# Attention: each V product as two products in 64-column halves of the array

## The chip, the cores and the metric

The kernel runs on one core of one Trainium2 chip. The metric is the time of one execution on the device in microseconds (us). Before the change two timed runs took 2069.55 and 2069.77 us (median 2069.66).

## The reference

Three stages follow one another. Attention with a block-causal mask of 64 tokens, over 4 batches, 8 heads, 576 tokens and 64 dimensions per head, feeds a layer with a cosine gate, and that feeds eight experts with a Sinkhorn gate. The change touches only the attention:

```python
def _attn_ref(q, k, v):
    B, H, S, D = q.shape                       # 4, 8, 576, 64
    scores = np.matmul(q, k.transpose(0, 1, 3, 2)) / np.sqrt(D)
    ...                                        # mask: block of the query >= block of the key
    scores = scores - np.max(scores, axis=-1, keepdims=True)
    attn = np.exp(scores)
    attn = attn / (np.sum(attn, axis=-1, keepdims=True) + 1e-09)
    return np.matmul(attn, v)
...
x = _moe_ref(x=attention rows, w_in, w_out)    # g = h * cos(h)
return _moe2_ref(x=x, w_gate, w1, w2)          # 8 experts, all of them for every token
```

## The kernel before

The order of all work is written out by hand; each engine runs its instructions in the order of the program. Attention is a loop over the 32 heads (`for i in range(NH)`, L445) and takes the first 191 us. Keys lie on the partitions, in five chunks of 128, and queries on the free axis, so that a product of scores gives, for one chunk of keys, a tile keys x queries. In head i TensorE does, in this order:

- the first part of the row maxima of head i + 1 (`peak`, L291, tile `px`), from rounded q and k;
- the scores of head i (`scores`, L330 and L331, tiles `sp`, `sq`, `sr`, `sc`), which ScalarE turns into weights with exp (L344, tiles `ep`, `eq`, `er`, `ec`);
- `pv(i, 0)`, the V product of the first chunk: two products, of 320 and 256 queries;
- the second part of the maxima (L291 again, two products);
- `pv(i, 1)` and `pv(i, 2)`: products of 128, 320 and 320 queries;
- the transpose of the maxima of head i + 1 (L318, tile `pt`), which waits for VectorE's reductions (L313);
- `pv(i, 3)` and `pv(i, 4)`: products of 192 and 64 queries.

So the V products of a head come in three groups, and between the groups TensorE does products that use the full width of the array. The moving operand of a V product is a tile of weights after exp (keys x queries), the stationary operand is V of that chunk, and the output is (dimension x queries), in PSUM tile `o`, of which there is one buffer. All of it is float32. The scores and everything after the attention run in a rounded form of float32 (`F32R`), with high and low parts.

The sums of the softmax come out of the same product. For an even head the stationary operand is 65 columns wide: V in columns 0 to 63, ones in column 64. For an odd head it is 128 wide: ones in column 0, zeros in 1 to 63, V in 64 to 127. So the output of an even head lies on partitions 0 to 63 with the sums on 64, and that of an odd head on 64 to 127 with the sums on 0; two heads then fill one tile of 128 partitions. `evac` (L360) copies output and sums to SBUF on ScalarE in the next head, before `pv(i, 0)` writes `o` anew.

After the attention there are narrow operands on TensorE too: the products for the gate (L551 and L552, tile `plt`, stationary operand 16 columns wide on 128 rows, rounded float32), a transpose of one column (L968, tile `pmx`, float32) and transposes on 16 rows (L559, tile `plg`, float32). `ones` (L51) is a tile of 128 x 128 ones that is made at the start.

Of the kernel before, what the change touches and what calls it, by code (L numbers as in the profile page):

```python
# [20 lines left out]
B, H, S, D = 4, 8, 576, 64  # L21
# [22 lines left out]
def attention_moe_kernel(ctx: ExitStack, tc: tile.TileContext, qk, v, w_a, gate, w_b, out):  # L44
    nc = tc.nc
# [5 lines left out]
    ones = top.tile([128, 128], F32, name="ones")  # L51
# [100 lines left out]
    def attention():  # L152
        with tc.tile_pool(name="at1", bufs=1) as p1, tc.tile_pool(name="at2", bufs=2) as p2, \
# [16 lines left out]
            V = [p1.tile([128, 5, D + 1], F32, name="v0"), p1.tile([128, 5, 2 * D], F32, name="v1")]  # L170
            VC = [slice(0, D), slice(D, 2 * D)]
# [9 lines left out]
            st, EP, EQ, ER, EC, SUMS, SR, INV, ps_t, ps_o = ({} for _ in range(10))  # L181
# [162 lines left out]
                nc.scalar.activation(E[i], ps[:, 0:n], AF.Exp, scale=0.125)  # L344

            def pv(i, c):
                m = D + 1 if i % 2 == 0 else 2 * D
                if c == 0:
                    ps_o[i] = pso.tile([128, 1024], F32, tag="o", name="o")
                o = ps_o[i][0:m, 256:832]  # L350
                vt = V[i % 2][:, :, 0:m]
                blocks = ((lambda: ((256, 576, EP[i][:, 0:320]), (0, 256, EQ[i][:, 0:256]))),
                          (lambda: ((128, 256, ER[i][:, 0:128]), (256, 576, ER.pop(i)[:, 128:448]))),
                          (lambda: ((256, 576, EC.pop(i)),)),
                          (lambda: ((384, 576, EP.pop(i)[:, 320:512]),)),
                          (lambda: ((512, 576, EQ.pop(i)[:, 256:320]),)))[c]()
                for q0, q1, e in blocks:
                    nc.tensor.matmul(o[:, q0:q1], vt[:, c], e, start=c == 0, stop=True, skip_group_check=c > 0)  # L358

            def evac(i):  # L360
                o, t = ps_o.pop(i)[:, 256:832], RAW[i // 2 % 3]
# [83 lines left out]
            for i in range(NH):  # L445
# [24 lines left out]
                if i % 4 == 2:  # L470
                    some(1)
                pv(i, 0)
                if nxt:
                    find(*peak(i + 1, 1))
# [17 lines left out]
                if i >= NH - 3:  # L492
                    j = i - (NH - 3)
                    f, o = FIRST[j][0], FIRST[j][1] * DM
                    split(*SPARE[j], raw[f][:, o:o + DM], nc.scalar, nc.gpsimd)
                pv(i, 1)
                pv(i, 2)
                if nxt:
                    turn(i + 1)
# [9 lines left out]
            e = NH - 2  # L509
# [7 lines left out]
    with tc.manual_schedule():  # L517
# [795 lines left out]
        tgen, at = None, ""  # L1313
# [11 lines left out]
        for g in range(NG + 2):  # L1325
            now, w = g < NA, Weights(g + 1) if g + 1 < NA else None
            left = NE * NJ - g % (NE * NJ)
            if left == 14 and g + left < NG:
                tgen = tprep(groups[g + left][0], nc.gpsimd)
                at = "sum"  # L1330
# [32 lines left out]
            if now:  # L1363
                if g:
# [3 lines left out]
                c = [fin.tile([128, TB], F32, tag=f"c{i}", name="c") if g else C01[i] if i < 2 else  # L1368
                     post.tile([128, TB], F32, tag="tt", name="c", bufs=3) for i in range(3)]
# [103 lines left out]
```

## Time and profile before

| | |
|---|---|
| timed runs | 2069.55 and 2069.77 us |
| span of the profiled execution | 2069.4 us |
| TensorE (PE) busy, its weight loads (PEld) | 2057.5 us, 1939.8 us |
| VectorE (DVE), ScalarE (ACT), GpSimd (POOL) busy | 1552.5, 1045.1, 830.2 us |
| attention stage | 0 to 191 us |
| line 358 (the V products) in the chain that ended last | 4% of the span |

The profile is of one execution, and times are counted from its first instruction. PE are products, PEld the weight loads ahead of them, which overlap the products. A product's start is measured and its end is modelled, so how long it holds the array is read from the start of what follows it. A float32 product appears as two records, each with a weight load of its own. In a row, `o<-ep,v` says that tile `o` is written from tiles `ep` and `v`; `128*65` is rows x columns of the stationary operand, and `128x320` partitions x elements of the moving one.

### The profile page before, as it was taken

What the parts mean: (1) busy time and instruction counts of PE and PEld (TensorE: products, weight loads), DVE (VectorE), ACT (ScalarE), POOL (GpSimd) and SP (SyncE); (2) the same over time, 40 slices, a digit from 0 to 9 for tenths busy, and PEclk for the clock granted to TensorE, in tenths of its full rate; (3) what the DMA queues carried; (4) which work ended last, traced back from release to release, by engine and by line L of the source; (5) the groups of instructions that cost most, each with busy time, mean ns of one, the idle gap of its engine ahead of it and who ended that gap; (6) DMA issues with size and microseconds to landing.
All of it is one profiled execution on the core that took longest, in us unless ns stands there. A gap on an engine that the chain in (4) does not pass through costs nothing.

```text
span 2069.4 us, 34729 instructions
## 1 busy us (share of the span) xinstructions
PE 2057.5 (99%) x12687; PEld 1939.8 (94%) x12687; DVE 1552.5 (75%) x2731; ACT 1045.1 (51%) x1852; POOL 830.2 (40%) x633
## 2 busy tenths in 40 slices
PE   9999999999999999999999999999999999999998
PEld 8888999999999898889889999999999999999998
DVE  7887786566668788887776777777777777777777
ACT  7887775434454433334333544454445444444443
POOL 4553332333325444455441333344444333333333
PEclk9999999999999999999999999999999999999999
DMA  6774330001035477766567455545555655455553
GB/s 163 186 187 130 117 98 1 6 1 41 1 106 205 160 256 246 255 237 220 204 221 248 165 200 177 207 165 201 179 203 183 210 177 204 165 204 176 197 173 112
DMA packets 177754, 340.89 MB, mean 165 GB/s; under 512 B 42128, under 2 KB 86672, under 8 KB 177584
## 3 DMA queue, kind: packets, MB, share of 16 engines
q1 hardware_dynamic: 177584, 338.68, 48.9%
q8 instruction: 100, 1.64, 0.3%
q14 instruction: 70, 0.57, 0.1%
HBM read 249.11 MB, written 80.36 MB: 159 GB/s over the span
## 4 chain that ended last, share of the span: by engine, by line
PE 92%; issue 4%; POOL 2%; DVE 1%; ACT 0%; POOLq 0%; DVEq 0%; ACTq 0%
PE p L524 8%; PE p L523 7%; PE p L522 7%; PE acc L805 7%; PE hx L522 6%; PE hx L523 6%; PE hx L524 6%; PE acc L522 4%; PE acc L524 4%; PE acc L523 4%; PE o L358 4%; PE hy L522 3%; PE hy L523 3%; PE hy L524 3%; PE h L522 2%
## 5 line engine op out<-in xcount | busy, mean ns | idle before, releaser
L1096 POOL TENSOR_TENSOR w<-s,w 128x512 fp32r<-128x512 f32 x150 | 236.6, 1578 | 408.2 <-ACT w L1095 394.9
L1192 DVE SCALAR_TENSOR_TENSOR oa<-p,P,oa 128x256 f32<-128x256 f32 x648 | 280.7, 477 | 69.5 <-PE p L524 67.9
L524 PE MATMUL p<-w,xl 128*128 128x256 f32 x906 | 255.9, 282 | 1.0 <-DVE xl L1143 1.0
L522 PE MATMUL p<-w,xh 128*128 128x256 f32 x846 | 238.2, 282 | 2.5 <-DVE oa L1192 1.7
L523 PE MATMUL p<-w,xh 128*128 128x256 f32 x846 | 238.4, 282 | 0.0
L638 POOL TENSOR_TENSOR wv<-stg,wv 128x512 fp32r<-128x512 f32 x62 | 111.0, 1811 | 232.1 <-ACT wv L637 225.1
L1096 POOL TENSOR_TENSOR w<-raw,w 128x512 fp32r<-128x512 f32 x74 | 116.6, 1576 | 188.7 <-ACT w L1095 175.5
L524 PEld LDWEIGHTS p<-w,xl 128*128 128x128 f32 x906 | 171.8, 190 | 1.5 <-DVE xl L1143 1.4
L759 POOL TENSOR_TENSOR jl<-raw,jh 128x512 fp32r<-128x512 f32 x63 | 92.3, 1465 | 189.6 <-ACT jh L754 169.6
L522 PEld LDWEIGHTS p<-w,xh 128*128 128x128 f32 x846 | 159.8, 189 | 2.9 <-issue 1.9
L523 PEld LDWEIGHTS p<-w,xh 128*128 128x128 f32 x846 | 160.3, 189 | 0.0
L522 PE MATMUL acc<-wv,hs 128*128 128x512 f32 x384 | 152.9, 398 | 0.0
L524 PE MATMUL acc<-wv,hs 128*128 128x512 f32 x384 | 152.0, 396 | 0.0
L523 PE MATMUL acc<-wv,hs 128*128 128x512 f32 x384 | 151.6, 395 | 0.0
L522 PE MATMUL p<-w,xl 128*128 128x256 f32 x498 | 140.0, 281 | 0.1
L523 PE MATMUL p<-w,xl 128*128 128x256 f32 x498 | 140.1, 281 | 0.0
L1040 DVE SCALAR_TENSOR_TENSOR oa<-acc,P,oa 128x512 f32<-128x512 f32 x168 | 123.8, 743 | 13.4 <-PE acc L524 13.4
L522 PE MATMUL hx<-th,w 128*128 128x384 f32 x384 | 129.6, 338 | 0.7 <-ACT c L1264 0.7
L523 PE MATMUL hx<-tl,w 128*128 128x384 f32 x384 | 129.0, 336 | 0.0
L524 PE MATMUL hx<-th,w 128*128 128x384 f32 x384 | 128.9, 336 | 0.0
L1139 ACT ACTIVATE xh<-raw 128x768 fp32r<-128x768 f32 x141 | 117.6, 843 | 17.3 <-DVE raw L1155 8.5
L524 PE MATMUL p<-w,xh 128*128 128x256 f32 x438 | 123.7, 282 | 0.6 <-DVE xh L1143 0.6
(309 smaller groups left out, 6367.7 us busy)
## 6 DMA issues: line engine op xcount, KB each, us to landing
w<-w1d SPq DMA_DIRECT2D x128, 512.0 KB
w<-w1d SPq DMA_DIRECT2D x128, 384.0 KB
stg<-in_w_b_dram SPq DMA_DIRECT2D x64, 512.0 KB
s<-td SPq DMA_DIRECT2D x86, 256.0 KB
w1d<-wah SPq DMA_DIRECT2D x32, 512.0 KB
w1d<-wal SPq DMA_DIRECT2D x32, 512.0 KB
s<-in_w_b_dram SPq DMA_DIRECT2D x64, 256.0 KB
td<-stg SPq DMA_DIRECT2D x52, 256.0 KB
```

The source lines that it names most:

```text
L358: nc.tensor.matmul(o[:, q0:q1], vt[:, c], e, start=c == 0, stop=True, skip_group_check=c > 0)
L522: nc.tensor.matmul(ps, lh, rh, start=first, stop=False, skip_group_check=go_on)
L523: nc.tensor.matmul(ps, lh, rl, start=False, stop=False, skip_group_check=go_on)
L524: nc.tensor.matmul(ps, ll, rh, start=False, stop=last, skip_group_check=go_on)
L638: eng.tensor_tensor(out=t[:, DM:2 * DM], in0=src, in1=t[:, 0:DM].bitcast(F32), op=ALU.subtract)
L759: eng.tensor_tensor(out=lo, in0=raw[units[n][1]][:, part * DM:(part + 1) * DM], in1=hi.bitcast(F32), op=ALU.subtract)
L805: nc.tensor.matmul(acc[half, b][:, at:at + w_], w[:, s], h[:, t0:t0 + w_], start=f == 0 and i == 0 and at == 0, stop=f == F1 - 1 and i == ...
L1040: nc.vector.scalar_tensor_tensor(out=o, in0=acc, scalar=p, in1=o, op0=ALU.mult, op1=ALU.add)
L1096: nc.gpsimd.tensor_tensor(out=t[:, DM:2 * DM], in0=raw, in1=t[:, 0:DM].bitcast(F32), op=ALU.subtract)
L1139: nc.scalar.activation(self.h[o], self.get(o), AF.Copy)
L1192: nc.vector.scalar_tensor_tensor(out=o, in0=ps, scalar=p, in1=o, op0=ALU.mult, op1=ALU.add)
```

## The change

A product of V is split in two that stream the same moving weights. One has V as its stationary operand, 64 columns, and writes the half of the partitions where the output of that head belongs (0 to 63 for an even head, 64 to 127 for an odd one). The other has 64 columns of `ones` and writes the other half, so that all 64 partitions of that half hold the sums. `evac` is unchanged and reads one of them. The output tile, the blocks and the groups stay as they are. What fills the columns of ones and zeros beside V is still there but no longer read.

```diff
             def pv(i, c):
-                m = D + 1 if i % 2 == 0 else 2 * D
                 if c == 0:
                     ps_o[i] = pso.tile([128, 1024], F32, tag="o", name="o")
-                o = ps_o[i][0:m, 256:832]
-                vt = V[i % 2][:, :, 0:m]
+                o = ps_o[i][:, 256:832]
+                at, of = ((0, D), (D, 2 * D)) if i % 2 == 0 else ((D, 2 * D), (0, D))
+                vt = V[i % 2][:, :, VC[i % 2]]
...
                 for q0, q1, e in blocks:
-                    nc.tensor.matmul(o[:, q0:q1], vt[:, c], e, start=c == 0, stop=True, skip_group_check=c > 0)
+                    nc.tensor.matmul(o[at[0]:at[1], q0:q1], vt[:, c], e, start=c == 0, stop=True,
+                                     skip_group_check=True)
+                    nc.tensor.matmul(o[of[0]:of[1], q0:q1], ones[:, 0:D], e, start=c == 0, stop=True,
+                                     skip_group_check=True)
```

On TensorE, the second and third group of an even head, with the transpose of the maxima between them; `v_109` is the tile of V of the even heads, and a shape is output partitions x queries:

```order
-L358 MATMUL o<-er,v_109 65x128
-L358 MATMUL o<-er,v_109 65x320
-L358 MATMUL o<-ec,v_109 65x320
+L358 MATMUL o<-er,v_109 64x128
+L360 MATMUL o<-er,ones 64x128
+L358 MATMUL o<-er,v_109 64x320
+L360 MATMUL o<-er,ones 64x320
+L358 MATMUL o<-ec,v_109 64x320
+L360 MATMUL o<-ec,ones 64x320
 L318 MATMUL pt<-ident,nm_107 101x128
```

Behind each product with V there is now one with `ones` on the same moving tile (line 360 of the changed kernel). The transpose comes after six products in place of three.

On TensorE, the first group of an odd head, between the last scores and the second part of the maxima; `v_110` is the tile of V of the odd heads:

```order
 L331 MATMUL sc<-qa_100,ka 128x320
-L358 MATMUL o<-ep,v_110 128x320
-L358 MATMUL o<-eq,v_110 128x256
+L358 MATMUL o<-ep,v_110 64x320
+L360 MATMUL o<-ep,ones 64x320
+L358 MATMUL o<-eq,v_110 64x256
+L360 MATMUL o<-eq,ones 64x256
 L291 MATMUL px<-ka,qa_99 128x448
```

Two products over all 128 partitions became four over 64, and a full-width product stands ahead of the group and behind it. No other engine's order changes.

## Rows read from the trace of the kernel before

**Rows 1.** The page, busy time of each engine: us, share of the span, records.
```profile
PE 2057.5 (99%) x12687; PEld 1939.8 (94%) x12687; DVE 1552.5 (75%) x2731; ACT 1045.1 (51%) x1852; POOL 830.2 (40%) x633
```
**Rows 2.** One stretch of the attention: PE, PEld, DVE, ACT, POOL busy; clock, DMA, GB/s.
```profile
50.00:90.00 40.00, 40.00 (x236) 32.91 (x234) 32.76 (x63) 33.06 (x61) 21.14 (x21) 1.00 0.71 187
```
**Rows 3.** Waits on PE's side, 0 to 192 us: total us, times, longest.
```profile
PEld pt L318 <- DVE nm L313: 11.3, 31, 0.4
...
PEld sp L331 <- DVE qa L322: 1.5, 2, 1.0
```
**Rows 4.** The chain that ended last, one head: start us, us, line, records.
```profile
42.64 0.97 PE o L358 x4
...
43.96 1.30 PE o L358 x6
...
45.43 0.49 PE o L358 x4
...
48.24 0.97 PE o L358 x4
```
**Rows 5.** Line 358 by shape, 0 to 192 us: records, busy us, mean ns, idle before.
```profile
L358 PEld LDWEIGHTS o<-er,v 128*128 128x128 f32 x64 | 9.0, 191 | 0.3
...
L358 PEld LDWEIGHTS o<-er,v 128*65 128x65 f32 x64 | 7.9, 137 | 0.4
...
L358 PE MATMUL o<-ec,v 128*128 128x320 f32 x32 | 11.2, 433 | 0.0
L358 PE MATMUL o<-ec,v 128*65 128x320 f32 x32 | 11.2, 433 | 0.0
```
**Rows 6.** V products in order of time, one even head: start us, us, records.
```profile
59.31 0.70 PE L358 MATMUL o<-ep,v 128*65 128x320 f32 x2
59.85 0.59 PE L358 MATMUL o<-eq,v 128*65 128x256 f32 x2
...
60.63 0.92 PE L358 MATMUL o<-er,v 128*65 128x128 f32 x4
61.38 0.70 PE L358 MATMUL o<-ec,v 128*65 128x320 f32 x2
...
62.09 0.49 PE L358 MATMUL o<-ep,v 128*65 128x192 f32 x2
62.42 0.28 PE L358 MATMUL o<-eq,v 128*65 128x64 f32 x2
```
**Rows 7.** Weight loads in order of time, the same head.
```profile
60.06 0.41 PEld L291 LDWEIGHTS px<-ka,qa 68*128 68x128 f32 x2
...
61.99 0.25 PEld L358 LDWEIGHTS o<-ep,v 128*65 128x65 f32 x2
...
62.48 0.55 PEld L291 LDWEIGHTS px<-ka,qa 68*128 68x128 f32 x4
```
**Rows 8.** Products in order of time: from the gate, 16 columns wide, to full width.
```profile
404.47 0.34 PE L552 MATMUL plt<-xl,gz 128*16 128x384 f32 x1
404.65 0.51 PE L805 MATMUL acc<-hh,jh 128*128 128x512 f32 x2
```
**Rows 9.** Products in order of time: from full width to one column.
```profile
616.81 0.34 PE L524 MATMUL hz<-xh,wbl 128*128 128x384 f32 x1
616.98 0.27 PE L968 MATMUL pmx<-ident,sm 128*1 128x128 f32 x1
```
**Rows 10.** Around the transposes on 16 rows: products, then weight loads.
```profile
611.96 0.33 PE L524 MATMUL hy<-xh,wal 128*128 128x384 f32 x1
612.22 0.35 PE L559 MATMUL plg<-ident,lt 16*128 16x16 f32 x3
612.43 0.33 PE L559 MATMUL plg<-ident,oa 16*128 16x16 f32 x3
...
612.22 0.26 PEld L559 LDWEIGHTS plg<-ident,lt 16*128 16x128 f32 x3 [0.25 <-issue]
...
612.80 0.19 PEld L523 LDWEIGHTS hx<-xl,wbh 128*128 128x128 f32 x1
```

## The prediction

> **What bounds the kernel now.** I read four views, from the widest to the closest. The page comes first: TensorE (PE) is busy for 99% of the span of 2069.4 us [rows 1]. A busy PE need not be a PE that bounds, so the second view is the attention stage alone, where the change lies: from 50 to 90 us PE is busy for all of the 40 us, VectorE (DVE) for 32.8, ScalarE (ACT) for 33.1 and GpSimd (POOL) for 21.1; the granted clock is 1.00, the 2.4 GHz level [rows 2]. Third, the waits of the first 192 us: PE's weight loads wait for VectorE 11.3 us, in 31 loads before the transposes of L318, and the next largest wait on PE's side is 1.5 us [rows 3]. So in this stage PE sets the pace, and what is added to it comes out at the end one for one. Fourth, the chain of work that ended last runs through PE in these heads. A head takes 5.6 us (42.64 to 48.24), and in it line 358 has three pieces, of 0.97, 1.30 and 0.49 us [rows 4]. That is 2.76 of 5.6 us in the line that the change doubles.
>
> **What one product costs.** Line 358 has 14 records per head in PE and 14 in the weight loads, for 7 products: each float32 product is two passes, a weight load and a product each, and there are 448 of each in the stage (32 heads; each row of a shape counts 16 heads x 2) [rows 5]. How long a pass holds the array is read from starts, since the ends are modelled. With 320 moving columns two passes start 0.54 us apart (59.31 to 59.85), so one is 0.27; 192 columns take 0.33 for two (62.09 to 62.42), 0.163 each; the four passes of L358 from 60.63 to 61.38 are two of 128 and two of 320, so 128 columns take 0.11. For 256 and 64 the following weight load tells it, which begins with the last pass: 59.85 to 60.06, 0.21, and 62.42 to 62.48, 0.06 [rows 6, 7].
>
> What matters most here: the duration of a pass does not depend on how many columns of the array are used. 320 moving columns are 433 ns on 65 columns and 433 on 128 [rows 5]. Halving the width of the weights makes a pass no shorter. Only the load gets shorter, from 191 to 137 ns when it falls from 128 to 65 columns [rows 5], and the loads lie under the pass before.
>
> **The change part by part.**
> 1. Removed: nothing from PE's stream. The V product keeps its two passes of the same moving columns.
> 2. Added: 7 products, 14 passes, on ones per head. One after the other they cost 2 x (0.27 + 0.21 + 0.11 + 0.27 + 0.27 + 0.163 + 0.06) = 2.71 us per head, within 0.05 of the three pieces of the chain; over 32 heads 86.7 us.
> 3. Weight loads: 14 more per head, of 64 columns, some 0.05 us of array time each (54 ns less for 63 columns fewer [rows 5] is 0.86 ns per column). The shortest pass is 0.06, so they stay covered. If they lost that cover, 28 loads of 0.054 per head would be 48 us.
> 4. Change of shape: three times per head PE goes from full-width products to halves and back, 96 times in all. The trace has narrow stationary operands already, with different answers. Of the gate products (16 columns, all 128 rows, 384 moving) the last starts at 404.47 and the next full-width product at 404.65 [rows 8]; 0.18 is within 0.01 of the step from one full-width 384 product to the next (0.17, 616.81 to 616.98 [rows 9]). The float32 transpose of a single column, in its turn, starts that same 0.17 after the full product ahead [rows 9]. Their price, out and in, is 0. The transposes on 16 rows pay: without a gap they would start at 612.13 (611.96 + 0.17), but the load begins at 612.22 after 0.25 idle; with its 0.06 that is 0.15 late. Behind them, three begin from 612.43 on in steps of 0.06 and would be over at 612.62; the next full product streams from 612.80, when the load after its own begins: 0.18 late. Together 0.33 per visit [rows 10], and 96 visits would be 32 us. The halves are narrow in columns and keep all rows, as the first two do, so I take 0 and keep 32 us for the range.
> 5. The wait before L318's load: the reduction of L313 ends so late that the transpose streams from 61.99, when the load behind it begins, and not from 61.92, when the array was free (61.38 + 2 x 0.27) [rows 6, 7]. With PE later, that 0.07 per head goes: -2 us over 31 heads.
> 6. ACT, DVE, POOL and the DMA queue keep every instruction in its order; the sums are read from the same partition as before. They have almost 7 us or more in 40 to spare [rows 2], and the single output buffer is written again only after the scores of the next head, 2.3 us behind the last V product (45.43 + 0.49 to 48.24 [rows 4]). Price 0; what would uncover them is a faster PE, not a slower one.
>
> Whether the two halves run at once decides the rest. No two products on different columns of the array stand in this trace, so it is bounded: nothing shared (86.7 us), or all that the order allows. That order is V first pass, V second, ones first, ones second; the two passes of one half need the same columns, so ones first can at best run beside V second, and ones second beside the next V first. Then a group takes each width twice as before, and the last ones pass of each group stands alone: where widths differ the longer counts. For the groups (320, 256), (128, 320, 320) and (192, 64) that adds 0.27, 0.27 and 0.16 us, 0.70 per head, 22.5 us in all. So even perfect sharing loses something, because one full-width product did both jobs already. I take the unshared end: in the groups of line 358 each pass starts only when the one before has streamed, and no row shows two at once [rows 6].
>
> Sum: 2069.4 + 86.7 - 2 = 2154.1, made against the span of the profiled execution; the two timed runs are 2069.55 and 2069.77, 0.3 us above it, so about **2154.5** in their terms.
>
> The Trainium skill, page "TensorEngine Tiling (Array Packing)", section "Key Properties", says that tiles load and multiply in parallel, and that a change of tiling mode drains TensorE. The trace bears out a drain in the 16-row transposes and shows none in the two column-narrow cases; of parallel tiles no run here shows anything. By the first half of the rule the time would be the overlap case below, by the second the drain case.
>
> **The rivals.**
> - *The halves overlap, no drain* (the other side: not slower by 2%). 2069.7 + 22.5 = 2092, or 2090 with the saved wait. For it: the two halves write different partitions and use different columns. Against: nothing in the rows. It decides if the ones pass starts with, and not after, V's second pass; the limit of 2%, 41 us or about 2111, which is what a measurement of this kernel can tell from no change, is passed once about a third of the 64 us between 22.5 and 86.7 is lost. Chance 0.15; partly overlapped, between 2111 and 2150, another 0.06.
> - *Each change of shape drains PE*, at 0.33 us as in [rows 10]. With overlap 2092 + 32 = 2124 (0.13); without it 2154.5 + 32 = 2186.5 (0.19). For it: the same data type and a changed shape. Against: [rows 8, 9].
> - *The loads lose their cover* in the narrow form. Then 28 x 0.054 us x 32 = 48 us come on top: 2203, and 2235 with the drain. For it: in the 16-row transposes load and product take turns, six in 0.06 us steps [rows 10]. Against: the gate products keep the step of full-width ones [rows 8]. Chance 0.09. The Trainium skill, "TensorE: Matmul & The Clock Gate", Part 3, section "The mechanism", says that loads overlap running products only when the row groups differ, and here they never do; the full-width rows of this trace go against it, since the load behind the pair of 256 begins at 60.06, with the second of them, and not at its end [rows 6, 7].
> - *Faster*: a 64-column product would have to need one pass in place of two. The equal durations at 65 and 128 columns speak against it. Chance 0.02.
>
> **How the numbers follow.** The forecast, one half after the other with covered loads and no drain, has 0.36 and its own range of 2145 to 2160. The range given reaches down to the full overlap (2090) and up past the drain without overlap (2186.5) to 2200; outside it are the uncovered loads and the faster case, 0.11. Slower by over 2%: 0.36 + 0.06 + 0.13 + 0.19 + 0.09 = 0.83. Within 2%: 0.15. Faster: 0.02.
>
> **What would show it.** In the changed profile, lines 358 and 360 should have 448 products each, with the old durations; the chain should show line 358 and 360 with 5.4 us of a head of 8.3, and the stage should end near 276 us in place of 191. In the starts of one group: V, V, ones, ones each 0.27 apart for 320 columns means no sharing; two that start within some 10 ns mean sharing; a first load after px or pt that begins only when the stream is over means a drain; loads that begin 0.05 before their own product, and not with the one before, mean lost cover. The prediction is wrong if the passes of one half get shorter, or if PE gets gaps whose releaser is another engine.

## The result

The changed kernel takes 2094.51 us (2094.42 and 2094.60 in two runs) against 2069.66: a ratio of 1.012, interval 1.0091 to 1.015. It is 24.9 us slower, less than the 2% over which the prediction had 0.83 of its chances. The direction was right and the size was not: 84.8 us were forecast. The time lies inside the given range, and near the 2092 of the first rival, but not for that rival's reason, as the trace shows.

The page of the changed kernel, PE's line, and one stretch of the attention in the columns of [rows 2]. The stage now ends 23.4 us later in the trace (the last V product starts at 214.3 in place of 190.9):

```profile
PE 2079.5 (99%) x13135; PEld 1926.3 (92%) x13135; DVE 1554.8 (74%) x2731; ACT 1046.3 (50%) x1852; POOL 830.0 (40%) x633
...
50.00:90.00 40.00, 40.00 (x295) 27.34 (x293) 31.02 (x59) 29.58 (x55) 17.67 (x17) 1.00 0.62 165
```

PE is busy for all 40 us as before, with 295 records of products in place of 236, and the others have more to spare: PE still sets the pace, and the clock is unchanged. What the busy share does not say is that two products run at a time. That stands in the order of time. The first group of an odd head in the changed kernel, products first, then weight loads (start us, us):

```profile
63.90 0.31 PE L330 MATMUL sc<-qb,kb 128*128 128x320 f32 x1
64.05 0.30 PE L331 MATMUL sc<-qa,ka 101*128 101x320 f32 x1
64.28 0.48 PE L358 MATMUL o<-ep,v 128*64 128x320 f32 x1
64.29 0.48 PE L360 MATMUL o<-ep,ones 128*64 128x320 f32 x1
64.60 0.43 PE L358 MATMUL o<-ep,v 128*64 128x320 f32 x1
64.61 0.43 PE L360 MATMUL o<-ep,ones 128*64 128x320 f32 x1
64.87 0.38 PE L358 MATMUL o<-eq,v 128*64 128x256 f32 x1
64.88 0.38 PE L360 MATMUL o<-eq,ones 128*64 128x256 f32 x1
65.09 0.38 PE L358 MATMUL o<-eq,v 128*64 128x256 f32 x1
65.09 0.38 PE L360 MATMUL o<-eq,ones 128*64 128x256 f32 x1
65.40 0.61 PE L291 MATMUL px<-ka,qa 68*128 68x448 f32 x2
```
```profile
63.90 0.19 PEld L331 LDWEIGHTS sc<-qa,ka 101*128 101x128 f32 x1
64.28 0.13 PEld L358 LDWEIGHTS o<-ep,v 128*64 128x64 f32 x1 [0.19 <-ACT eq L344]
64.29 0.13 PEld L360 LDWEIGHTS o<-ep,ones 128*64 128x64 f32 x1
64.34 0.14 PEld L358 LDWEIGHTS o<-ep,v 128*64 128x64 f32 x1
...
65.40 0.30 PEld L291 LDWEIGHTS px<-ka,qa 68*128 68x128 f32 x2 [0.38 <-issue]
...
65.51 0.19 PEld L291 LDWEIGHTS px<-ka,qa 68*128 68x128 f32 x1
```

Two things are to be seen. First, the order is V, ones, V, ones: each pass on ones starts within 0.01 us of the same pass on V (0.005 to 0.007 in all 448 pairs of the stage), and the next pair follows after 0.27 (64.60 to 64.87), the time of one pass in [rows 6]. The second pass on ones has no slot of its own at the end. Second, the group begins and ends with a stall. The last score product (L331) would be over 0.15 after its start, at 64.20; the load of V begins at 64.28 only, and its product streams from 64.34, when the load of its second pass begins: 0.14 late. The last pair would be over at 65.09 + 0.21 = 65.30; the load of `px` begins at 65.40 and its product streams with the next load at 65.51: 0.21 late. Before, the same `px` product streamed on time (the second load of the pair that begins at 60.06 in [rows 7] stands 0.22 behind, when the pass of 256 columns was over). And at the way in, in the kernel before, the load of V began with the score product ahead, and the product 0.15 behind it, on time:

```profile
59.16 0.31 PE L331 MATMUL sc<-qa,ka 101*128 101x320 f32 x1
...
59.18 0.27 PEld L358 LDWEIGHTS o<-ep,v 128*65 128x65 f32 x2
```

The waits on the side of the weight loads, 0 to 217 us, in the form of [rows 3], show the same stalls under other names:

```profile
PEld pt L318 <- DVE nm L313: 15.2, 31, 0.5
PEld px L291 <- issue: 12.2, 31, 0.7
PEld o L358 <- ACT qa L260: 7.3, 30, 0.2
PEld o L358 <- ACT eq L344: 6.1, 32, 0.2
```

The two rows of `o` are new, and that of `px` was 1.1 us in two waits. The releasers ACT and "issue" are what came last by the profile, not what was waited for. ScalarE is the obvious suspect for the first group; its rows in the head shown:

```profile
63.33 0.57 ACT L344 ACTIVATE ep<-sp 128x512 f32<-128x512 f32 x1
63.81 0.41 ACT L344 ACTIVATE eq<-sq 128x320 f32<-128x320 f32 x1
```

The tile that the first V product reads, `ep`, is ready at 63.90, 0.38 before the load. `eq`, which the profile names, ends 0.06 before the load in this head and 0.10 before it in its neighbours, while the load begins 0.084 to 0.086 after the array has run empty in thirty heads in a row; and in the kernel before the same load began 0.13 to 0.27 ahead of the end of `eq`. So the load follows the empty array, not ScalarE. Idle time of the loads is no sum of lost time, since part of it was hidden before.

Over 25 heads in the middle of the stage I took the mean steps between four kinds of starts. From the last score product to the second `px` product it is 1.663 us after and 1.325 before, 0.34 more; from there to the transpose 0.23 more; from the transpose to the next head's first score 0.28 more; the scores themselves 0.04 less. That is 0.81 per head, 26 us if all 32 heads were alike. Counted from the first V load (13.67 us before, 12.17 after) to the start of the last V product (190.93 and 214.35), the stage is 24.9 us longer, as measured. That the two ends lie 23.4 apart, as the spans do, comes from the start of that one execution of the kernel before: its first score products of 320 columns are 0.26 us apart (12.53 to 12.79), those of the changed kernel 0.16 (10.68 to 10.84), and neither had reached a V product by then.

### The profile page after: what moved, and what is told of

Read it like the earlier page. It is cut to its first block, busy times and chain, and to the rows that moved or that the text cites. A ratio compares the mean times of both kernels' runs of the same rounds, so it can differ in the third digit from the quotient of the medians.

```text
span 2092.8 us, 35625 instructions
## 1 busy us (share of the span) xinstructions
PE 2079.5 (99%) x13135; PEld 1926.3 (92%) x13135; DVE 1554.8 (74%) x2731; ACT 1046.3 (50%) x1852; POOL 830.0 (40%) x633
## 4 chain that ended last, share of the span: by engine, by line
PE 89%; issue 6%; POOL 3%; DVE 1%; DMA 1%; ACT 0%; SPq 0%; POOLq 0%; DVEq 0%; ACTq 0%
PE p L527 7%; PE p L526 7%; PE p L525 7%; PE acc L808 7%; PE hx L525 6%; PE hx L526 6%; PE hx L527 6%; PE o L358 5%; PE acc L525 4%; PE acc L527 4%; PE acc L526 4%; PE hy L525 3%; PE hy L526 3%; PE hy L527 3%; PE h L525 2%
```

## The experiments

Two theories stood against each other after the result. **A**: the halves run side by side, pass by pass, and the loss is the price of 96 visits to another shape (a visit: into the halves and out again). **B**: the overlap rival of the prediction, one pass behind, with a lone pass at the end of each group and no price of shape. Line numbers in the rows are those of each experiment's own file.

**Is it sharing?** Chunks 1 to 4 with both products in the same half, V replaced by zeros, so that the output lacks V of these chunks:

```diff
-  nc.tensor.matmul(o[at[0]:at[1], q0:q1], vt[:, c], e, ...)
+  half = at if c == 0 else of
+  nc.tensor.matmul(o[half[0]:half[1], q0:q1], vt[:, c] if c == 0 else zeros_w, e, ...)
   nc.tensor.matmul(o[of[0]:of[1], q0:q1], ones[:, 0:D], e, ...)
```

> In the second and third group of each head (chunks 1 to 4) both products of a pair go to the same half of the array: the V product is replaced by a product of zeros in the half of the sums, so the output lacks V of these chunks. Number, width and shape of all products stay those of the changed kernel. Theory A (the halves run side by side, and the 25 us are the price of the changes of shape): the pairs of these groups lose their sharing, 2 x (0.11 + 0.27 + 0.27 + 0.163 + 0.06) = 1.75 us per head, 56 us in all: 2094.5 + 56 = 2150.5. Rival B (the overlap rival of the prediction: the second half runs one pass behind the first, the last pass of a group alone, no price for the shape): the first group keeps its 0.27 per head, the others run bare: 2069.7 + 8.6 + 56 = 2134. Rival C (no sharing at all): no change, 2094.5.

Measured: 2149.33 us (2149.09 to 2151.11), 54.8 over the changed kernel, where A had 56 and B 2134. The rows of its second group, products in order of time:

```profile
64.88 0.43 PE L361 MATMUL o<-er,zeros_w 128*64 128x128 f32 x2
65.15 0.38 PE L363 MATMUL o<-er,ones 128*64 128x128 f32 x2
65.36 0.70 PE L361 MATMUL o<-er,zeros_w 128*64 128x320 f32 x2
65.90 0.70 PE L363 MATMUL o<-er,ones 128*64 128x320 f32 x2
```

In one half two products of 320 columns are 0.54 apart (65.36 to 65.90), one behind the other, with their loads covered; that is what the prediction took for all pairs. In two halves they share the time. So a pass behind another in its own half costs full price, and a pass in the other half nothing to speak of.

**Is the second product free?** The V product of chunks 1 to 4 left out:

```diff
-  nc.tensor.matmul(o[at[0]:at[1], q0:q1], vt[:, c], e, ...)
+  if c == 0:
+      nc.tensor.matmul(o[at[0]:at[1], q0:q1], vt[:, c], e, ...)
   nc.tensor.matmul(o[of[0]:of[1], q0:q1], ones[:, 0:D], e, ...)
```

> In the second and third group of each head (chunks 1 to 4) only the product on ones is left, the V product of these chunks is left out. The changes of shape stay, 96 visits. Theory A: the V product ran beside the one on ones and cost nothing but the step between the two, so the time stays within 1 us of 2094.5. Rival B: the passes that stand alone at the end of the second and third group go, 0.27 + 0.16 us per head, 14 us: 2080.5. Rival C (no sharing): 56 us less, 2038.

Measured: 2093.84 us (2093.80 to 2096.38), 0.7 under the changed kernel. Five of seven V products per head are gone and the time is the same; B and no sharing are both out. What remains, the 24 us, is there although the second and third group have no pair left to run.

**What does one visit cost by itself?** One small product per head in the kernel before, at the head of the first group, on 64 columns of ones and on 128:

```diff
+  nc.tensor.matmul(ps_o[i][0:64, 832:896], ones[:, 0:64], EP[i][:, 0:64], start=True, stop=True)
   o = ps_o[i][0:m, 256:832]
```

> The kernel before, and in each head one extra product of 64 moving columns at the head of the first V group, with 64 columns of ones, into unused columns of the output tile. That is one visit to the halved shape per head, with nothing beside it. Theory A: against the same with 128 columns of ones, one visit dearer, 0.26 us per head by the total of 25 us over 96 visits, 8 to 10 us in all: 2082. Rival B: no difference between the two.

> The control of the run before: the same extra product on 128 columns of ones, so that the shape never changes. Both theories: two passes of 0.06 us per head, at most 0.11 each where the load of 128 columns is not covered: 3.8 to 7 us, 2073.5 to 2077.

Measured: 2082.88 us (2082.64 to 2083.65) with 64 columns and 2075.66 (2075.45 to 2077.30) with 128. The narrower product is 7.2 us dearer, 0.23 us per visit, a little under the 8 to 10 expected of A. Products and loads of visit_64:

```profile
60.51 0.31 PE L331 MATMUL sc<-qa,ka 101*128 101x320 f32 x1
60.76 0.33 PE L350 MATMUL o<-ep,ones 128*64 128x64 f32 x2
61.01 0.75 PE L359 MATMUL o<-ep,v 128*65 128x320 f32 x2
```
```profile
60.75 0.19 PEld L350 LDWEIGHTS o<-ep,ones 128*64 128x64 f32 x2 [0.20 <-issue]
61.01 0.19 PEld L359 LDWEIGHTS o<-ep,v 128*65 128x65 f32 x2
```

The scores would be over at 60.66 and the load begins at 60.75, so the product streams from 60.81, 0.15 late; its two passes of 0.053 would be over at 60.92, the load back to full width begins at 61.01 and its product streams from 61.07, 0.15 late again. That is the picture of the changed kernel with nothing beside it. The gross price of this visit is 0.30 us (0.14 + 0.21 in the first group above, where a load of 128 columns stands behind it and not one of 65), and with the two passes it makes 0.41 per head, 13 us, against the 12.9 by which the run is over the kernel before. The difference of the two runs is smaller because the control pays too, by loads of 128 columns that a pass of 64 columns does not cover.

**Why did the gate products show no price?** They are narrow (16 columns) and of the rounded type. One run has 16 columns in plain float32, two have 64 and 128 columns in the rounded type:

```diff
+  nc.tensor.matmul(ps_o[i][0:16, 832:896], ones[:, 0:16], EP[i][:, 0:64], start=True, stop=True)
```

> As visit_64, with 16 columns of ones in place of 64, plain float32. If the type decides and not the width, the visit costs as with 64 columns: 2082.9 within 1 us. If the width does (16 columns as the gate products have them, no price), the time of visit_128 or a little under it, 2074 to 2076.

Measured: 2081.40 us (2081.13 to 2081.93), 11.1 us over the kernel before, where visit_64 has 12.9 and visit_128 5.7. The visit stays dear. Of the 1.8 us less than visit_64 some 1.3 are the shorter load, by an estimate: the product streams 0.015 us after its load begins in place of 0.055, 32 times. Its loads:

```profile
60.78 0.11 PEld L350 LDWEIGHTS o<-ep,ones 128*16 128x16 f32 x2 [0.19 <-issue]
61.00 0.19 PEld L359 LDWEIGHTS o<-ep,v 128*65 128x65 f32 x2
```

The first pair in the rounded type used the head's own q and k (the control has `QB[i % 2][:, 0:128]` and all 128 partitions of the output):

```diff
+  for h in range(2):
+      nc.tensor.matmul(ps_o[i][0:64, 832:1024], QB[i % 2][:, 0:64],
+                       KBP[:, i % 2 * KP:i % 2 * KP + 192], start=True, stop=True)
```

> The kernel before, with two extra products per head ahead of the first V group, in the rounded form of float32 (one pass), 64 columns of stationary operand and 192 moving ones, into unused columns of the output tile. It asks why the gate products of the kernel before showed no price for a narrow operand: because of their rounded type, or because of their width. If the type decides, the loads begin under the product ahead and the time is that of the control below within 1 us. If any operand of 64 columns changes the shape, one visit per head, 0.23 us as measured with visit_64, some 7 us over the control.

> The control of the run before: the same two products per head with 128 columns. One pass of 192 columns is 0.08 us at the rate of 448 columns in 0.20, and the load of 128 columns is the longer at 0.11: 2 x 0.08 to 2 x 0.11 per head, 5 to 7 us, 2075 to 2077.

Measured: 2257.83 and 2259.52 us. These two tell nothing on the question: by the program's order the tiles are already those of head i + 2 at that place, so the products waited for a DMA (`PE o L351 <- DMA kb<-qb`, 111.9 us in all in the first 400), and a stall of that size hides any price. They were made anew on the next head's keys, which have been in place since the head before (128 columns in the control, again):

```diff
+      nc.tensor.matmul(ps_o[i][0:64, 832:1024], KBP[:, (i + 1) % 2 * KP:(i + 1) % 2 * KP + 64],
+                       KBP[:, (i + 1) % 2 * KP:(i + 1) % 2 * KP + 192], start=True, stop=True)
```

> The comparison of rounded_64 and rounded_128 again, on operands that nothing waits for: both are the high and low parts of the next head's keys, which are there since the head before. Two extra products per head in the rounded form of float32, 64 columns of stationary operand, 192 moving. If the type decides, every load begins under the product ahead, and the time is that of ahead_128 within 1 us or less by the shorter loads, 2 x 0.03 us per head, 2 us. If any operand of 64 columns changes the shape, some 7 us over ahead_128.

> The control: the same two products on 128 columns. One pass of 192 columns is 0.08 us and the load of 128 columns 0.11: 2 x 0.08 to 2 x 0.11 us per head, 5 to 7 us, 2075 to 2077.

Measured: 2078.21 us (2077.14 to 2078.51) with 64 columns, 2079.72 (2079.51 to 2080.07) with 128. The narrow one is 1.5 us faster, by its loads, and pays no visit. Products and loads of ahead_64:

```profile
62.66 0.31 PE L331 MATMUL sc<-qa,ka 101*128 101x320 f32 x1
62.80 0.34 PE L351 MATMUL o<-kb 128*64 128x192 f32 x2
62.98 0.70 PE L361 MATMUL o<-ep,v 128*65 128x320 f32 x2
```
```profile
62.66 0.29 PEld L351 LDWEIGHTS o<-kb 128*64 128x64 f32 x2
62.89 0.23 PEld L361 LDWEIGHTS o<-ep,v 128*65 128x65 f32 x2
```

The load of 64 columns begins at 62.66, with the score product ahead, and the products follow at 0.14 and 0.18, without a gap in or out. So at 64 columns the type decides the price: plain float32 pays and the rounded form does not. The two kinds of run also differ in their moving columns, 64 and 192, but the changed kernel pays with 64 to 320. That the rounded form keeps the full shape would explain it and is not shown: no run has two rounded products in different halves, so whether they would share is open.

**How far apart may a pair stand?** In each group all V products first, then all on ones:

```diff
-      nc.tensor.matmul(o[of[0]:of[1], q0:q1], ones[:, 0:D], e, ...)
+      late_ones.append((o[of[0]:of[1], q0:q1], e, c == 0))
+  if c in (0, 2, 4):
+      while late_ones:
+          out, e, first = late_ones.pop(0)
+          nc.tensor.matmul(out, ones[:, 0:D], e, start=first, stop=True, skip_group_check=True)
```

> The changed kernel, but in each group all V products come first and all products on ones behind them; nothing else is changed. It asks how far apart the two of a pair may stand. If a product can only run beside its neighbour in the program's order, a group shares only where its last V product meets its first one on ones: bare times are 0.54 + 0.54 + 0.42 against 0.96 in the first group, 2.38 against 1.30 in the second and 0.78 against 0.45 in the third, 1.95 us more per head, 62 us: 2157. If TensorE takes the products of the other half from further behind, 2094.5. Theory A allows both, rival B only the first.

Measured: 2103.23 us (2103.11 to 2104.90), 8.7 over the changed kernel: neither of the two answers. The rows of its first and second group tell why (L359 is V, L365 ones):

```profile
61.25 0.48 PE L359 MATMUL o<-ep,v 128*64 128x320 f32 x1
61.27 0.48 PE L365 MATMUL o<-ep,ones 128*64 128x320 f32 x1
```
```profile
62.92 0.70 PE L359 MATMUL o<-er,v 128*64 128x128 f32 x3
63.20 0.43 PE L365 MATMUL o<-er,ones 128*64 128x128 f32 x2
63.46 0.43 PE L359 MATMUL o<-er,v 128*64 128x320 f32 x1
63.47 0.43 PE L365 MATMUL o<-er,ones 128*64 128x320 f32 x1
63.73 0.43 PE L359 MATMUL o<-ec,v 128*64 128x320 f32 x1
63.74 0.43 PE L365 MATMUL o<-er,ones 128*64 128x320 f32 x1
64.00 0.43 PE L359 MATMUL o<-ec,v 128*64 128x320 f32 x1
64.00 0.70 PE L365 MATMUL o<-ec,ones 128*64 128x320 f32 x2
```

With two V products ahead, the first on ones starts beside the first V pass, past the second V product. With three ahead it starts at 63.20, when the first V product is over and the second begins. From there on everything is shared, and one pass of 320 columns stands alone at the end: 0.27 us per head, 8.7 us over 32, which is the whole difference. So in this stream a product went past one waiting product of the other half, not past two.

**Two visits in place of three.** The second part of the maxima moved ahead of the first group, in the changed kernel and in the one before:

```diff
+  if nxt:
+      find(*peak(i + 1, 1))
   pv(i, 0)
-  if nxt:
-      find(*peak(i + 1, 1))
```

> The changed kernel with the second part of the maxima issued ahead of the first V group, so that the first and second group stand together: two visits to the halved shape per head in place of three. Theory A: against the kernel before with the same order, 64 visits of 0.26 us, 16.6 us more. Rival B: a pass that stands alone after 320 columns and the steps between widths, and one after 192, 0.59 us per head, 19 us more.

> The control of the run before: the kernel before with the second part of the maxima ahead of the first V group. Both theories: the same work on TensorE, 2069.7 within 3 us, unless the reductions of the maxima come too late or ScalarE's weights were waited for.

Measured: 2093.40 us (2091.68 to 2093.58) and 2080.55 (2079.70 to 2081.28), 12.9 apart where A had 16.6 and B 19. (The lowest runs are 12.0 apart.) Both numbers were built on three visits of one price. The visit that is removed, out of the first group and into the second, is the dearest (0.21 + 0.14, with nothing to hide it before): 0.35 x 32 = 11.2 off the 24.9 leaves 13.7, near what was measured; but this was worked out after the fact, and the pair is no clean measure of two visits, since each has waits of its own, below. The order itself costs 10.4 us in the kernel before, which was not expected. There the chain that ended last now has a wait for VectorE in a head:

```profile
61.19 0.81 DVE nm L313 x2
62.00 0.14 issue
62.13 0.59 PE px L291 x2
```

The second `px` products need the buffer that the reductions of the first still read; the V products of the first group had covered that. PE has this wait 19 times in that kernel, 7.0 us in all, and 6 times in the changed one, 3.2 us. So the run shows no order that beats the kernel before; nor does any other run here.

## Why the prediction failed, step by step

Two steps failed, in opposite directions: the products on ones were put at 86.7 us and cost next to nothing, and the change of shape was put at nothing and cost the 24.9 us.

- *What bounds the stage*: right. PE set the pace before and after; every stall on it came out at the end.
- *A pass is no shorter for half the columns*: right. 320 columns are 0.27 apart in both kernels.
- *Step 2, 86.7 us for the products on ones, and "I take the unshared end"*: this step failed. The reason given was that the rows show no two products at once; but they had no two products in different halves either, so they could not have shown it. The bound from below, 22.5 us, was the nearer one, and even it was too high: same_half shows 54.8 us for five products of a head that lose their sharing, ones_only 0.7 us for the same five when they have it.
- *The order of passes in the overlap rival*: wrong too. It put the two passes of a product behind each other as one piece, and so had a lone pass in each group, 22.5 us. The trace has V, ones, V, ones: the first pass on ones runs ahead of V's second. The rival's 2092 is close to the measured 2094.5 by chance: its 22.5 us are not there, and the 24.9 us that are come from a step that it had at 0.
- *Step 4, the price of a change of shape, taken as 0*: this step failed. Of three cases in the trace I chose by the outline, narrow in columns with all rows, and took the gate products and the transpose of one column [rows 8, 9] for the nearest. The runs point to the type for the gate products: 16 columns in plain float32 pay (visit_16), 64 in the rounded form do not (ahead_64). Why the float32 transpose of a column [rows 9] pays nothing was not tried; its row counts one record (x1), where a plain float32 product has two, so it was no product of the same kind either. The bound from above, the transposes on 16 rows with 0.33 per visit [rows 10], fits the gross price of 0.14 + 0.21, though they are narrow in rows and not in columns.
- *Its sum, 32 us for 96 visits*: a little high. Net of what the kernel before lost at the same places (the late transposes, loads that a pass of 64 columns does not cover) 0.81 us per head remain, 26 us.
- *Step 5, 2 us back at the transposes*: not seen as a gain. The wait is longer in the rows, 15.2 us against 11.3 [rows 3], since the transpose now stands behind a change of shape. What the kernel before lost there is in the net price above.
- *"0.3 us above it" in the sum*: it compared two executions. A timed run is 1.8 us above the span of its own execution (2094.60 and 2092.8), so by an estimate the profiled one of the kernel before took 2071.2; this moves the forecast by less than 2 us.
- *Loads lose their cover*: no. Within a group every load begins with the pass before it; only the first of a group and the first behind it are bare.
- *The Trainium skill, "TensorEngine Tiling (Array Packing)", "Key Properties"*: both halves of the rule hold here, tiles in parallel (0.01 us between the starts of a pair) and a drain at the change of mode (0.14 in, 0.21 out), with the limit that the runs put to it: operands of 64 columns in the rounded form show no such price. The rule of the Trainium skill, "TensorE: Matmul & The Clock Gate", Part 3, "The mechanism", that the prediction named, on loads that overlap only with other row groups, does not hold in these rows as it was put there: at 64.34 the load of V's second pass begins while its first streams, on the same rows. The same section excepts a load into the background weight buffer, and no run here shows whether these loads go there.

The case that held was the drain with overlap, given 0.13 and 2124; without its tail of 22.5, and with the 24.9 us that the stage grew in the trace in place of 32, it comes to 2069.7 + 24.9 = 2094.6.

## What to carry to other kernels

Two float32 products in different column halves of the array cost the time of one, so splitting a product that already used the full width for both jobs can gain nothing, and the way into the halves and out again is paid, here 0.30 to 0.35 us gross per visit. What follows from it, though no run here tried such a kernel: use halves where the array would otherwise stand half empty, in long runs without full-width products between them, with the two of a pair next to each other in the program (v_then_ones lost 8.7 us by taking them apart). And where a trace has several rows near to a new operation, compare data type and mode before outline; a row in which a thing could not have happened is no evidence that it doesn't.

## What the runs showed of the hardware beyond that

- A pair in two halves shares pass by pass, and its two loads run side by side too (64.28 and 64.29, 0.13 us each).
- A product of the other half was taken past one waiting product and not past two (v_then_ones, 0.27 us per head).
- The stall on the way in does not depend on the width, only the load behind it does: 16 and 64 columns in plain float32 both begin their load about 0.09 us after the array has run empty (60.75 against 60.66 in visit_64; 60.78 against 60.70 in visit_16, where the last score product starts at 60.55).
